# Linear attention and GLU layers on one core: attention read out token by token, key normalization and LayerNorm apply on GpSimd, GLU weights kept, next keys and values emitted between GLU slabs

## The chip, the core and the metric

The kernel runs on one core of one Trainium2 chip. The metric is the device time of one execution in microseconds (us), as a median of several runs. The profile adds the span of one execution, which is some 2 us shorter than the time. Its engines are PE (TensorE products; PEld is its weight load), DVE (VectorE), ACT (ScalarE), POOL (GpSimd) and SP (which issues most DMA transfers).

## The reference

Four layers on 2048 tokens of 512 columns: attention, GLU, attention, GLU, each with a LayerNorm in front and a residual sum behind. Cut to what matters:

```python
# A: 32 heads of 16 columns, linear attention with a softmax feature map
pq, pk = q @ w_phi, k @ w_phi                       # per head, 16x16
phi_q = concat(softmax(pq), softmax(-pq))           # 32 features a head
phi_k = concat(softmax(pk), softmax(-pk))
kv, z = phi_k.T @ v, phi_k.sum(tokens)              # over all tokens
out = (phi_q @ kv) / (phi_q @ z + 1e-6)  ...  @ wo
# B: GLU, F = 1376
h = relu(x @ W_gate) * (x @ W_up);  out = h @ W_down
# layers: x = x + A(ln(x)); x = x + B(ln(x)); twice
```

The sum over all tokens in `kv` is the barrier in an attention layer: no token can be read out before the last key is in.

## The kernel before

The program lists operations with what they read and write and an assumed length. A list scheduler in the file fixes each engine's order from these lengths, before the kernel is built; on the chip every engine then runs its list strictly in order. Tokens come in 16 tiles of 128, or 4 slabs of 512. The parts that matter here (shortened, lambdas unwrapped):

```python
# LayerNorm of a tile: statistics, 1/sqrt by a Newton step, apply: all on DVE; then a DMA transpose
op("dve", tensor_scalar(ytile, x_sb[t], mv[t,0:1], rstd[t], op0=subtract, op1=mult), dur=340)    # L577
dma("sp", dma_start_transpose(yT[:, :, tile], ytile))
...
# keys: exp on ACT, group sums on DVE; VALUES are multiplied by 1/sum, mostly on GpSimd
op("pool", tensor_tensor(vhat[t,s], vsb, rZk[...].to_broadcast([P, 32, 16]), mult), dur=1250)    # L622
...
# query sums, feature-major: 32-column products, reciprocals, transposes, and a 512-column
# product that spreads each head's factor over its 16 rows; the same again for the denominator
op("pe", matmul(pb, EC[c], RT_sb[slab]), dur=216)                                                # L681
op("pe", matmul(pb, kvbd[0,c], expq[st,c,0]), ...); op("pe", matmul(pb, kvbd[1,c], expqm[st,c])) # L727, L729
op("pe", matmul(pb, EC[c], rdenT_sb[slab]), dur=216)                                             # L731
...
# GLU: weights share memory with the attention's buffers and are loaded for each GLU layer
dma("sp", dma_start(Wg, B_W_gate)) ...
# ---- cut: setup, scheduler, semaphores
```

The softmax here doesn't subtract the row's maximum and nothing guards it: scores larger than these inputs give would overflow.

Of the kernel before, what the change touches and what calls it, by code (L numbers as in the profile page):

```python
# [269 lines left out]


class KB:

    def __init__(self, nc, A_x, A_wqkv, A_w_phi, A_wo, B_W_gate, B_W_up, B_W_down, out,
                 nlayers=4, debug_outs=None, dve_vhat_tiles=(2, 5, 7, 10, 13, 15), resid_on_pool=False, ot_mode="half", expqm_mode="half", nr_iters=1, ln_pre_emit=False, rstd_mode="dve", yt_copy_act="half", wcopy_act=True,
                 window=(("sp", 64), ("act", 96), ("pe", 300), ("dve", 24), ("pool", 32)), sched_params=(("SYNC_LAT", 500.0), ("SAME_LAT", 600.0))):
        self.dve_vhat_tiles = tuple(dve_vhat_tiles)
        self.resid_on_pool = resid_on_pool
        self.ot_mode = ot_mode
        self.expqm_mode = expqm_mode  # L280
        self.nr_iters = nr_iters
        self.ln_pre_emit = ln_pre_emit
        self.rstd_mode = rstd_mode
        self.yt_copy_act = yt_copy_act
        self.wcopy_act = wcopy_act
        self.nc = nc
        self.prog = Program(nc, window=dict(window))
        sp = dict(sched_params) if sched_params else {}
        if "SYNC_LAT" in sp:
            self.prog.SYNC_LAT = sp["SYNC_LAT"]  # L290
        if "SAME_LAT" in sp:
            self.prog.SAME_LAT = sp["SAME_LAT"]
        if "DMA_BW" in sp:
            self.prog.DMA_BW = sp["DMA_BW"]
        if "DMA_FIXED" in sp:
            self.prog.DMA_FIXED = sp["DMA_FIXED"]
        if "DMA_GLOBAL_Q" in sp:
            self.prog.DMA_GLOBAL_Q = sp["DMA_GLOBAL_Q"]
        self.A_x, self.A_wqkv, self.A_w_phi, self.A_wo = A_x, A_wqkv, A_w_phi, A_wo
        self.B_W_gate, self.B_W_up, self.B_W_down, self.out = B_W_gate, B_W_up, B_W_down, out  # L300
        self.debug_outs = debug_outs or {}
        self.nlayers = nlayers
        B, S, D = A_x.shape
        assert B == 1 and D == 512 and S % 512 == 0
        self.S = S
        self.NT = S // 128
        self.NSLAB = S // 512
        self.D = 512
        self.NC = 4
        self.H = 32  # L310
        self.DH = 16
        self.HF = 512
        self.F = B_W_gate.shape[1]
        assert self.F == 1376
        self.NFC = 11
        self.FLAST = self.F - 10 * 128
        self.eps_ln = 1e-5
        self.eps_den = 1e-6

    def op(self, eng, fn, reads=(), writes=(), dur=100.0, name=""):  # L320
        return self.prog.op(eng, fn, reads, writes, dur, name)

    def dma(self, eng, fn, reads=(), writes=(), nbytes=0, name=""):
        return self.prog.dma(eng, fn, reads, writes, nbytes, name)

    def build(self):
        nc = self.nc
        S, NT, NSLAB, NC, NFC = self.S, self.NT, self.NSLAB, self.NC, self.NFC
        with ExitStack() as ctx:
            E = ctx.enter_context  # L330
            self.sems = {e: E(nc.semaphore(f"sem_{e}")) for e in ENG_NAMES}
            self.dsems = [E(nc.semaphore(f"dsem{i}")) for i in range(self.prog.n_dma_sems)]

            x_sb = E(nc.sbuf_tensor("x_sb", [P, NT, 512], BF16))
            yT = E(nc.sbuf_tensor("yT", [P, NC, S], BF16))
            wv = E(nc.sbuf_tensor("wv", [P, NC, 512], BF16))
            Wqp = E(nc.sbuf_tensor("Wqp", [P, NC, 512], BF16))
            Wkp = E(nc.sbuf_tensor("Wkp", [P, NC, 512], BF16))
            wo_sb = E(nc.sbuf_tensor("wo_sb", [P, NC, 512], BF16))
            BD = E(nc.sbuf_tensor("BD", [P, NC, 128], BF16))  # L340
            ones_c = E(nc.sbuf_tensor("ones_c", [P, 4, 32], BF16))
            ident = E(nc.sbuf_tensor("ident", [P, 128], BF16))
            ident32 = E(nc.sbuf_tensor("ident32", [P, 128], FP32))
            EC2 = E(nc.sbuf_tensor("EC2", [P, 4, 32], BF16))
            EC2t = E(nc.sbuf_tensor("EC2t", [P, 4, 32], BF16))
            ones32 = E(nc.sbuf_tensor("ones32", [P, 4, 128], BF16))
            EC = E(nc.sbuf_tensor("EC", [P, 4, 128], BF16))
            eps_c = E(nc.sbuf_tensor("eps_c", [P, 1], FP32))
            stats6 = E(nc.sbuf_tensor("stats6", [P, NT, 6], FP32))
            mv = E(nc.sbuf_tensor("mv", [P, NT, 2], FP32))  # L350
            rstd = E(nc.sbuf_tensor("rstd", [P, NT, 1], FP32))
            rs_v1 = E(nc.sbuf_tensor("rs_v1", [P, NT, 1], FP32))
            rs_hx = E(nc.sbuf_tensor("rs_hx", [P, NT, 1], FP32))
            rs_t1 = E(nc.sbuf_tensor("rs_t1", [P, NT, 1], FP32))
            NYB = 6
            ytile = E(nc.sbuf_tensor("ytile", [P, NYB, 512], BF16))
            nA = max(NT * 2 * 512, 2 * NFC * 512, 6144)
            nB = max(NT * 2 * 544, 8 * 1376 + NFC * 512)
            nA = (nA + 511) // 512 * 512
            nB = (nB + 543) // 544 * 544  # L360
            regA = E(nc.sbuf_tensor("regA", [P, nA], BF16))
            regB = E(nc.sbuf_tensor("regB", [P, nB], BF16))
            vsb = E(nc.sbuf_tensor("vsb", [P, 2, 512], BF16))
            Zk = E(nc.sbuf_tensor("Zk", [P, 2, 64], FP32))
            NRZ = 4
            rZk = E(nc.sbuf_tensor("rZk", [P, NRZ, 64], FP32))
            kvbd = E(nc.sbuf_tensor("kvbd", [P, 2, NC, 128], BF16))
            kvden = E(nc.sbuf_tensor("kvden", [P, 2, NC, 32], BF16))
            expq = E(nc.sbuf_tensor("expq", [P, NSLAB, NC, 2, 512], BF16))
            expqm = E(nc.sbuf_tensor("expqm", [P, NSLAB, NC, 512], BF16))  # L370
            rz2tmp = E(nc.sbuf_tensor("rz2tmp", [P, 2, 4, 32], FP32))
            Rtok = E(nc.sbuf_tensor("Rtok", [P, 2, 4, 32], BF16))
            RT_sb = E(nc.sbuf_tensor("RT_sb", [P, S], BF16))
            rden_tmp = E(nc.sbuf_tensor("rden_tmp", [P, 2, 4, 32], FP32))
            rden_tok = E(nc.sbuf_tensor("rden_tok", [P, 2, 4, 32], BF16))
            rdenT_sb = E(nc.sbuf_tensor("rdenT_sb", [P, S], BF16))
            rdenb_sb = E(nc.sbuf_tensor("rdenb_sb", [P, 2, 512], BF16))
            oT = E(nc.sbuf_tensor("oT", [P, 2, NC, 512], BF16))
            numT_sb = E(nc.sbuf_tensor("numT_sb", [P, 2, 512], BF16))
            rbt_sb = E(nc.sbuf_tensor("rbt_sb", [P, 2, 512], BF16))  # L380

            gate_sb = E(nc.sbuf_tensor("gate_sb", [P, 3, 512], BF16))
            pb = [E(nc.psum_tensor(f"pb{i}", [P, 512], FP32)) for i in range(8)]
            pb16 = [pb[i][:].bitcast(BF16) for i in range(8)]
            R_pb = [Res(f"pb{i}", pe_ordered=True) for i in range(8)]

            expk = regA[:, 0:NT * 2 * 512].rearrange("p (t s n) -> p t s n", t=NT, s=2)
            hT = regA[:, 0:2 * NFC * 512].rearrange("p (b f n) -> p b f n", b=2, f=NFC)
            Wqnat = regA[:, 0:2048].rearrange("p (c n) -> p c n", c=4)
            Wknat = regA[:, 2048:4096].rearrange("p (c n) -> p c n", c=4)  # L390
            WT = regA[:, 4096:6144].rearrange("p (c n) -> p c n", c=4)
            vhat = regB[:, 0:NT * 2 * 544].rearrange("p (t s n) -> p t s n", t=NT, s=2)
            Wg = regB[:, 0:4 * 1376].rearrange("p (c n) -> p c n", c=4)
            Wu = regB[:, 4 * 1376:8 * 1376].rearrange("p (c n) -> p c n", c=4)
            Wd = regB[:, 8 * 1376:8 * 1376 + NFC * 512].rearrange("p (c n) -> p c n", c=NFC)

            R = {}

            def RR(key):
                r = R.get(key)  # L400
                if r is None:
                    r = R[key] = Res(str(key))
                return r
            nuA = nA // 512
            nuB = nB // 544
            RA = [Res(f"regA{u}") for u in range(nuA)]
            RB = [Res(f"regB{u}") for u in range(nuB)]

            def uA(e0, e1):
                return [RA[u] for u in range(e0 // 512, (e1 + 511) // 512)]  # L410

# [107 lines left out]
            def R_xall():  # L519
                return [R_x[t] for t in range(NT)]  # L520
# [387 lines left out]
```

## Time and profile before

| | before |
|---|---|
| time, median | 456.97 us (3 runs) |
| span of the profiled run | 453.7 us |
| first GLU product of the two GLU layers | 124.3 and 336.4 us |
| LayerNorm's (LN's) apply: subtract the mean, times 1/root; where and how long | DVE, 0.41 us |

The page first: busy time of each engine, then the busy share in 40 slices of 11.3 us, in tenths (PEclk is the granted TensorE clock), then the engines' shares of the chain that ended last.

```profile
span 453.7 us, 6812 instructions
...
PE 417.4 (92%) x2592; PEld 202.9 (45%) x2592; DVE 298.8 (66%) x696; ACT 174.8 (39%) x317; POOL 92.8 (20%) x128
...
PE   2598989899499999999999999989979999999997
...
DVE  4959984889974333368758999488997333343342
...
POOL 6008660654000000000002666056400000000000
...
PE 72%; DVE 18%; issue 3%; DMA 3%; ACT 2%; POOL 1%; SPq 1%; DVEq 0%; POOLq 0%
```

TensorE is busy for 92% of the span and makes 72% of the chain. GpSimd is idle in both GLU layers (the zeros in its row). The chain in order of time (start, length, engine and line) shows what a GLU layer looks like:

```profile
143.45 0.86 PE pb L779 x4
144.31 0.86 PE pb L782 x4
145.17 9.51 PE pb L794 x44
154.69 0.87 PE pb L779 x4
```

Four 512-column products take 0.86 us and the 44 down products of a slab 9.51, so 216 ns each. A slab takes 28.5 us with no gap, and the four of one layer 114. What can be won lies in the attention layers. The table of stretches (start and end, length, then busy us of PE, PEld, DVE, ACT, POOL with counts, granted clock, DMA) shows the readout of the first attention layer as its second row and a whole GLU layer as its third:

```profile
core 0: us, PE busy (x) PEld busy (x) DVE busy (x) ACT busy (x) POOL busy (x), PEclk, DMA share, GB/s
20.00:76.00 56.00, 52.09 (x385) 28.33 (x385) 44.01 (x98) 40.06 (x77) 24.50 (x40) 1.00 0.19 33
76.00:124.00 48.00, 39.16 (x373) 18.92 (x371) 43.38 (x102) 19.81 (x36) 18.35 (x16) 1.00 0.31 99
124.00:242.00 118.00, 117.67 (x538) 53.76 (x539) 65.18 (x165) 26.49 (x45) 0.00 (x0) 0.99 0.14 27
```

In the readout DVE is busy 43.4 of 48 us and TensorE 39.2. Two groups of instructions matter for later (line, engine, operation, output<-inputs, shapes, count, busy us, mean ns of one, idle time before):

```profile
L577 DVE TENSOR_SCALAR ytile<-x_sb,mv,rstd 128x512 bf16<-128x512 bf16 x64 | 22.7, 406 | 5.6 <-DMA yT<-ytile 5.5
...
L622 POOL TENSOR_TENSOR regB<-vsb,rZk 128x512 bf16<-128x512 bf16 x40 | 41.8, 1058 | 176.8 <-DVE rZk L613 162.5 <-ACT vsb L618 7.9 <-DVE regB L633 2.6
```

### The profile page before, as it was taken

The numbers are of one execution on the slowest core, as the hardware profiler recorded it, in microseconds if no ns is written. First come the engines' busy times: TensorE is split into PE (matmuls) and PEld (weight loads), VectorE is DVE, ScalarE is ACT, GpSimd is POOL, SyncE is SP. The second block draws the span as 40 slices with busy tenths as digits, with TensorE's granted clock in tenths as the row PEclk, the third lists the DMA queues.
The fourth block names the chain that finished last, engine by engine and source line by source line (L and its number), as shares of the span: only waits on it lengthen the run. The fifth ranks groups of instructions, "written<-read, shape, count | busy, mean of one in ns | idle before, by whom it ended". The sixth has DMA issues, their size and how long they took to land.

```text
span 453.7 us, 6812 instructions
## 1 busy us (share of the span) xinstructions
PE 417.4 (92%) x2592; PEld 202.9 (45%) x2592; DVE 298.8 (66%) x696; ACT 174.8 (39%) x317; POOL 92.8 (20%) x128
## 2 busy tenths in 40 slices
PE   2598989899499999999999999989979999999997
PEld 1243458443144444444444345745324444444443
DVE  4959984889974333368758999488997333343342
ACT  3488864445022131231315986435513123131230
POOL 6008660654000000000002666056400000000000
PEclk9999999999989999999999999999999999999999
DMA  8752003610233000002220200370023210100101
GB/s 275 154 94 36 1 1 105 216 58 0 46 72 69 0 2 0 1 0 48 47 46 1 46 1 1 127 237 15 0 56 73 59 48 0 46 1 0 48 1 46
DMA packets 46800, 23.59 MB, mean 52 GB/s; under 512 B 35824, under 2 KB 44720, under 8 KB 46768
## 3 DMA queue, kind: packets, MB, share of 16 engines
q1 hardware_dynamic: 45184, 21.59, 18.6%
q10 hardware_dynamic: 1584, 1.57, 1.0%
q8 instruction: 20, 0.33, 0.3%
q14 instruction: 12, 0.10, 0.1%
HBM read 12.66 MB, written 2.10 MB: 33 GB/s over the span
## 4 chain that ended last, share of the span: by engine, by line
PE 72%; DVE 18%; issue 3%; DMA 3%; ACT 2%; POOL 1%; SPq 1%; DVEq 0%; POOLq 0%
PE pb L779 17%; PE pb L782 17%; PE pb L794 17%; PE pb L604 4%; PE pb L653 4%; PE pb L640 3%; DVE Zk L610 3%; DVE x_sb L757 3%; PE pb L602 2%; DVE regB L630 2%; PE pb L748 2%; DVE stats L530 2%; DMA BD<-in_A_w_phi_dram 2%; DVE expqm L684 1%; PE pb L665 1%
## 5 line engine op out<-in xcount | busy, mean ns | idle before, releaser
L785 ACT ACTIVATE gate_sb<-pb 128x512 bf16<-128x512 f32 (+1 forms) x88 | 52.5, 597 | 176.4 <-PE pb L779 155.8
L787 DVE TENSOR_TENSOR regA<-gate_sb,pb 128x512 bf16<-128x512 bf16 (+1 forms) x88 | 60.3, 686 | 71.4 <-PE pb L782 68.9
L779 PE MATMUL pb<-yT,regB 128*128 128x512 bf16 (+1 forms) x352 | 90.9, 382 | 5.8 <-DMA yT<-ytile 5.8
L782 PE MATMUL pb<-yT,regB 128*128 128x512 bf16 (+1 forms) x352 | 90.9, 382 | 0.0
L622 POOL TENSOR_TENSOR regB<-vsb,rZk 128x512 bf16<-128x512 bf16 x40 | 41.8, 1058 | 176.8 <-DVE rZk L613 162.5
L794 PE MATMUL pb<-regB,regA 128*128 128x512 bf16 (+1 forms) x352 | 77.4, 379 | 0.0
L779 PEld LDWEIGHTS pb<-yT,regB 128*128 128x128 bf16 (+1 forms) x352 | 35.3, 101 | 47.8 <-issue 7.8
L782 PEld LDWEIGHTS pb<-yT,regB 128*128 128x128 bf16 (+1 forms) x352 | 35.5, 101 | 41.3 <-issue 1.1
L794 PEld LDWEIGHTS pb<-regB,regA 128*128 128x128 bf16 (+1 forms) x352 | 34.3, 98 | 41.5
L796 DVE TENSOR_TENSOR x_sb<-x_sb,pb 128x512 bf16<-128x512 bf16 x32 | 22.0, 687 | 46.6 <-PE pb L794 46.6
L530 DVE BATCH_NORM_STATS2 stats<-x_sb 128x6 f32<-128x512 bf16 x64 | 42.5, 671 | 6.3 <-DMA x_sb<-in_A_x_dram 6.3
L656 ACT ACTIVATE expq<-pb 128x512 bf16<-128x512 f32 x64 | 35.7, 613 | 19.9 <-PE pb L653 17.9
L607 ACT ACTIVATE regA<-pb 128x512 bf16<-128x512 f32 x64 | 35.0, 612 | 17.5 <-PE pb L602 17.5
L604 PE MATMUL pb<-wv,yT 128*128 128x512 bf16 x128 | 35.5, 395 | 3.4 <-DVE regB L630 3.3
L610 DVE TENSOR_REDUCE Zk<-regA 128x64 f32<-128x1024 bf16 x32 | 37.8, 1188 | 1.1 <-ACT regA L607 1.1
L748 PE MATMUL pb<-wo_sb,oT 128*128 128x512 bf16 x128 | 32.8, 380 | 5.3 <-DVE x_sb L757 5.3
L602 PE MATMUL pb<-Wkp,yT 128*128 128x512 bf16 x128 | 34.0, 379 | 0.4 <-ACT Wqp L513 0.2
L653 PE MATMUL pb<-yT,Wqp 128*128 128x512 bf16 x128 | 33.5, 379 | 0.0
L577 DVE TENSOR_SCALAR ytile<-x_sb,mv,rstd 128x512 bf16<-128x512 bf16 x64 | 22.7, 406 | 5.6 <-DMA yT<-ytile 5.5
L690 POOL TENSOR_TENSOR expqm<-expq,rbt_sb 128x512 bf16<-128x512 bf16 x16 | 18.5, 1155 | 35.9 <-ACT rbt_sb L688 35.9
L733 ACT ACTIVATE rdenb_sb<-pb 128x512 bf16<-128x512 f32 x32 | 18.4, 597 | 13.8 <-PE pb L731 7.1
L739 POOL TENSOR_TENSOR oT<-rdenb_sb,numT_sb 128x512 bf16<-128x512 bf16 x16 | 18.5, 1155 | 21.9 <-ACT numT_sb L737 15.0
(75 smaller groups left out, 427.2 us busy)
## 6 DMA issues: line engine op xcount, KB each, us to landing
regB<-in_B_W_gate_dram SPq DMA_DIRECT2D x2, 1376.0 KB, 6.0
regB<-in_B_W_up_dram SPq DMA_DIRECT2D x2, 1376.0 KB, 6.0
regB<-in_B_W_down_dram SPq DMA_DIRECT2D x2, 1280.0 KB, 7.0
x_sb<-in_A_x_dram SPq DMA_DIRECT2D x4, 512.0 KB, 9.0
out_dram<-x_sb SPq DMA_DIRECT2D x3, 512.0 KB, 2.9
regA<-in_A_wqkv_dram ACTq DMA_DIRECT2D x2, 512.0 KB, 7.1
yT<-ytile SPq DMA_TRANSPOSE x64, 2.5
wv<-in_A_wqkv_dram ACTq DMA_DIRECT2D x1, 512.0 KB, 11.1
```

The source lines that it names most:

```text
L530: op("dve", (lambda t: (lambda e: e.bn_stats(stats6[:, t, :], x_sb[:, t, :])))(t), reads=[R_x[t]], writes=[R_stats[t]], dur=620, name=f"{t ...
L602: op("pe", (lambda t, ic, bk_k: (lambda e: e.matmul(pb[bk_k][:], yT[:, ic, t * 128:(t + 1) * 128], Wkp[:, ic, :], start=(ic == 0), stop=(i ...
L604: op("pe", (lambda t, ic, bk_v: (lambda e: e.matmul(pb[bk_v][:], yT[:, ic, t * 128:(t + 1) * 128], wv[:, ic, :], start=(ic == 0), stop=(ic ...
L610: op("dve", (lambda t, zb: (lambda e: e.tensor_reduce(Zk[:, zb, :], expk[:, t, :, :].rearrange("p s (h f) -> p (s h) f", f=16), AX.X, ALU. ...
L622: op("pool", (lambda vh, vb, rb, s: (lambda e: e.tensor_tensor(vh[:, :, 0:16], vsb[:, vb, :].rearrange("p (h d) -> p h d", d=16), rZk[:, r ...
L653: op("pe", (lambda st, c, ic, bk: (lambda e: e.matmul(pb[bk][:], Wqp[:, ic, c * 128:(c + 1) * 128], yT[:, ic, st * 512:(st + 1) * 512], st ...
L748: op("pe", (lambda tt, c, bk, ob: (lambda e: e.matmul(pb[bk][:], oT[:, ob, c, tt * 128:(tt + 1) * 128], wo_sb[:, c, :], start=(c == 0), st ...
L779: op("pe", (lambda st, fc, Mf, ic, gb: (lambda e: e.matmul(pb[gb][0:Mf, :], Wg[:, ic, fc * 128:fc * 128 + Mf], yT[:, ic, st * 512:(st + 1) ...
L782: op("pe", (lambda st, fc, Mf, ic, ub: (lambda e: e.matmul(pb[ub][0:Mf, :], Wu[:, ic, fc * 128:fc * 128 + Mf], yT[:, ic, st * 512:(st + 1) ...
L785: op("act", (lambda Mf, gb, gsb: (lambda e: e.activation(gate_sb[0:Mf, gsb, :], pb[gb][0:Mf, :], ACT.Relu)))(Mf, gb, gsb), reads=[R_pb[gb] ...
L787: op("dve", (lambda Mf, ub, gsb, hb, fc: (lambda e: e.tensor_tensor(hT[0:Mf, hb, fc, :], gate_sb[0:Mf, gsb, :], pb[ub][0:Mf, :], ALU.mult) ...
L794: op("pe", (lambda hb, fc, Kf, tt, bk: (lambda e: e.matmul(pb[bk][:], hT[0:Kf, hb, fc, tt * 128:(tt + 1) * 128], Wd[0:Kf, fc, :], start=(f ...
```

## The change

The intent was to take products and DVE work out of the attention readout, and to hide the rest under the GLU, whose products leave the other engines free.

- The readout is token-major: for 128 tokens one product of 144 columns per group gives numerators, denominators and the query sums together. Six small DVE operations, one 1024-element product and a sum of two halves on GpSimd follow; then a DMA transpose in front of the output projection.
- Keys are divided by their sums in place of values, on GpSimd, 1024 elements a tile.
- LayerNorm's reciprocal root and its apply move from DVE to GpSimd.
- The GLU weights have memory of their own and are loaded once.
- The readouts of slabs 1 to 3 and the keys and values of the next attention layer are emitted between GLU slabs.
- The lengths that the scheduler assumes are new as well.

The diff, cut to its core:

```diff
-    op("dve", tensor_scalar(ytile, x_sb[t], mv[t,0:1], rstd[t], op0=subtract, op1=mult), dur=340)
+    op("pool", tensor_scalar(rv1[t], mv[t,1:2], EPS_LN, None, op0=add), 250)                 # L429
+    op("pool", tensor_tensor(rstd[t], rv1[t], mhalf, pow), 300)                              # L430
+    op("pool", tensor_scalar(ytile, x_sb[t], mv[t,0:1], rstd[t], op0=subtract, op1=mult), 600) # L432
 ...
-    op("pool", tensor_tensor(vhat[t,s], vsb, rZk.to_broadcast(...), mult))
+    op("pool", tensor_tensor(expk[t], expk[t], rZk.to_broadcast([P, 64, 16]), mult), 2100)   # L454
 ...
+  def num(t):
+    for g in 8 groups: op("pe", matmul(pb[144 columns], expq[...], kvbd[g]), 66)             # L507
+    op("act", copy to numbf) x3
+    op("dve", zm = tensor_tensor(numbf, numbf, mult), 100) x2                                # L517
+    op("dve", zd = tensor_tensor(zm, zm, add), 100);  op("dve", zr = reciprocal(zd), 330)    # L520, L521
+    op("dve", ab = tensor_tensor(numbf, zr, mult), 100) x2                                   # L523
+    op("dve", tsc = tensor_tensor(numbf, ab.to_broadcast, mult), 620)                        # L527
+    op("pool", osb = tensor_tensor(tsc[0:512], tsc[512:1024], add), 1100)                    # L532
+    dma_start_transpose(oT, osb);  4 x matmul(pb, oT, wo_p);  x_sb += pb                     # L538
 ...
+    N(0); q_proj(1..3); N(1); Bf(0); N(2); Bf(1); N(3); K(0); Bf(2); K(1); Bf(3); K(2) ...
 ---- cut: setup, weight loads, the end
```

## The prediction

> **What bounds it now.** TensorE, in two GLU layers that are packed and two attention layers that are not. In the chain of waits a GLU slab ticks without a gap: 22 groups of four 512-column products at 0.86 us, then 44 down products in 9.51 us: 216 ns each, the warm figure of the Trainium skill ("TensorE: Matmul & The Clock Gate", "Back-to-back issue gap"); 28.5 us a slab, 228 us for both layers. That cannot shrink. The other 220 us: attention until the first GLU product at 124.3 us, and again from about 240 to 336. There the stretch table shows DVE busy 43.4 of the 48 us from 76 to 124, TensorE 39.2.
>
> **Removed.** The 512-column broadcasts of sums (64) and numerators (64): 128 x 216 ns = 28 us of TensorE; 512 32-column products, 64 small transposes; ACT copies of broadcasts, 128x128 reciprocals (0.95 us), DVE's rstd chain and LN apply (0.41 us x64). The second GLU weight load is off the path.
>
> **Added.** 256 144-column products replace the numerators: about 62 ns each, estimated from 59 ns for 136 columns (96 in 5.69 us). Estimated TensorE floor: 1568 x 0.216 + 256 x 0.057 + 16 + 2 = 371 us. On DVE per tile six small ops of 0.15-0.35 us and one 1024-element product, about 0.65 us by "VectorE: DVE Perf Modes", "Rules for kernel authors" (2x on tensor_tensor, bf16 in SBUF); no run yet shows it. GpSimd gets LN's rstd and apply (estimate 1.2 us a tile, from its 0.52 us 128x512 memset and 0.3 us small ops) and the key product, 2 x 1.06 = 2.1 us a tile, from the 128x512 product with a broadcast operand. 32 more DMA transposes (1.27 us issue, 2.5 us to landing) lie between numerator and output projection.
>
> **Moved.** Later readouts go between GLU slabs, three quarters of layer 3's keys and values into and behind slabs 2 and 3. Only the first slab's readout stays exposed.
>
> **The sum (estimates).**
> - Start: weight transposes hold the DMA issuer; first projection about 20 us, before 18.6: no gain.
> - First keys/values: GpSimd bound, 16 x 3.3 us; the issuer is full too. Readout factors ready at about 72; before, the last key product ran at 75.
> - First readout: product, copy, DVE, GpSimd, transpose, projection, LN, transpose, four tiles: 23 us. GLU starts at 95 (before 124).
> - GLU with interleaved work: 114 + 3.5 + 5.5 + 5.5 + 14 = 142, stalls 3: 240. Layer 3 starts when it did, with half its keys done.
> - Eight GpSimd key products in series (17 us) plus latency: factors at 265; readout 21: GLU at 286 (before 336).
> - GLU 128, stalls 3, store 4: span 421; the time is 2 us above the span.
>
> **Predicted: 423 us, 80% range 406 to 440.** Faster by over 2% 0.93, within 2% 0.05, slower 0.02.
>
> **Right if:** GLU's first product comes at 90-100 us and again at 278-295; GpSimd busy rises from 93 to 170-200 us, over 85% between 25 and 70 us and after 243; the key product takes 2.0-2.2 us; the chain of waits goes through GpSimd in those two stretches; a GLU slab with a readout in it takes 33-36 us.
>
> **Wrong if:** GpSimd's one-column power or apply is far over 0.3 and 0.6 us, or the key product slows against DVE; small dependent DVE ops cost over 0.3 us each and stretch the readout; with four banks for gate and up and in-order engines, TensorE stands behind output projections whose inputs are late, losing several us in each of six mixed slabs (towards 440); or start-up is quicker than I think (towards 406).

## The result, and the profile after

The changed kernel gives the right result and takes 487.47 us (485.96 to 487.80, 4 runs), against 456.62 for the kernel before. The ratio is 1.067, 95% interval 1.064 to 1.070: slower by 6.7%, where faster by 7% was predicted. Ratios here are the mean time of one kernel's runs over that of the other's of the same rounds, so not quite the ratio of the medians that are quoted. Executions over 1.5% slower than the fastest of the same kernel are left out of the means. The lines that answer to those of before:

```profile
span 485.6 us, 5893 instructions
...
PE 403.8 (83%) x2112; PEld 192.9 (40%) x2112; DVE 271.2 (56%) x580; ACT 182.1 (38%) x353; POOL 288.2 (59%) x271
...
PE   1626986874999979996689999895699998998997
...
DVE  2731634586742953895366464587563783593342
...
POOL 5999998359560282589999188529490164156000
PEclk9975988996799999999799999997699998999999
...
PE 48%; POOL 32%; DVE 8%; DMA 6%; issue 4%; ACT 3%; ACTq 0%; POOLq 0%
```

TensorE is less busy and DVE too, as intended. GpSimd rose from 92.8 to 288.2 us, far over the predicted 170 to 200, and holds 32% of the chain, where it had 1%. Its row shows nines from the second slice to the sixth, 12 to 73 us. The stretches:

```profile
core 0: us, PE busy (x) PEld busy (x) DVE busy (x) ACT busy (x) POOL busy (x), PEclk, DMA share, GB/s
22.00:84.00 62.00, 41.29 (x226) 20.28 (x225) 24.97 (x33) 26.59 (x51) 60.69 (x51) 0.81 0.39 103
84.00:121.00 37.00, 25.25 (x163) 12.38 (x161) 25.84 (x71) 23.76 (x51) 22.78 (x20) 0.89 0.14 29
121.00:156.00 35.00, 34.81 (x153) 15.65 (x154) 18.02 (x34) 6.97 (x12) 13.73 (x14) 0.92 0.15 31
194.00:240.00 46.00, 36.63 (x179) 16.51 (x177) 29.86 (x75) 16.25 (x32) 37.63 (x38) 0.93 0.19 38
```

From 22 to 84 us GpSimd is busy for 60.7 of 62 us and no other engine is busy for more than 41.3. TensorE idles there, and its granted clock drops to a mean of 0.81. The Trainium skill ("TensorE: Matmul & The Clock Gate", "Part 1: The HAM clock gate") says that the array's clock is cut to half after it stood idle and is restored after some us of work; the trace agrees. The same view in finer stretches, where the first GLU begins:

```profile
117.00:121.00 4.00, 0.00 (x0) 0.00 (x0) 2.15 (x5) 0.56 (x2) 3.79 (x3) 0.50 0.18 37
...
124.00:127.00 3.00, 3.00 (x10) 1.11 (x9) 2.00 (x6) 0.00 (x0) 1.15 (x1) 0.59 0.22 44
127.00:130.00 3.00, 3.00 (x16) 1.35 (x15) 2.65 (x7) 0.60 (x1) 0.63 (x2) 1.00 0.22 44
```

After an idle stretch the clock stands at 0.50, and some 5 us into steady work it is back at 1.00. So the low clock follows from the waiting, and lengthens the first products after it.

The groups of GpSimd, and the one DVE operation that stands out:

```profile
L432 POOL TENSOR_SCALAR ytile<-x_sb,mv,rstd 128x512 bf16<-128x512 bf16 x64 | 133.7, 2092 | 4.5 <-POOL rstd L430 1.6
...
L454 POOL TENSOR_TENSOR expk<-expk,rZk 128x1024 bf16<-128x1024 bf16 x32 | 61.1, 1926 | 7.9 <-DVE rZk L453 7.9
...
L430 POOL TENSOR_TENSOR rstd<-rv,mhalf 128x1 f32<-128x1 f32 x64 | 36.4, 573 | 3.8
...
L520 DVE TENSOR_TENSOR zd<-zm 128x32 f32<-128x32 f32 x32 | 13.3, 415 | 0.6
```

The LN apply takes 2.09 us a tile. I priced it at 0.6 us, and so did the scheduler. It alone is 133.7 us of GpSimd. The chain of waits just before the first GLU product reads:

```profile
110.04 2.09 POOL ytile L432
...
112.41 0.58 POOL rstd L430
...
113.08 2.14 POOL ytile L432
...
115.51 0.58 POOL rstd L430
...
116.18 2.39 POOL ytile L432
...
118.59 2.46 DMA yT<-ytile
```

One apply follows the other every 3.1 us, and only then come the transpose (2.46 us) and the GLU.

### The profile page after: what moved, and what is told of

It is laid out like the page before. It is cut to its first block, busy times and chain, and to the rows that moved or that the text cites. A ratio compares the mean times of both kernels' runs of the same rounds, so it can differ in the third digit from the quotient of the medians.

```text
span 485.6 us, 5893 instructions
## 1 busy us (share of the span) xinstructions
PE 403.8 (83%) x2112; PEld 192.9 (40%) x2112; DVE 271.2 (56%) x580; ACT 182.1 (38%) x353; POOL 288.2 (59%) x271
## 4 chain that ended last, share of the span: by engine, by line
PE 48%; POOL 32%; DVE 8%; DMA 6%; issue 4%; ACT 3%; ACTq 0%; POOLq 0%
PE pb L554 23%; POOL ytile L432 17%; PE pb L568 13%; POOL expk L454 5%; PE pb L443 5%; POOL rstd L430 5%; PE pb L538 3%; DMA oT<-osb 3%; POOL osb L532 2%; POOL rv L429 2%; PE pb L491 2%; DMA yT<-ytile 2%; DVE zd L520 1%; ACT expq L494 1%; DMA hT<-in_A_wqkv_dram 1%
## 5 line engine op out<-in xcount | busy, mean ns | idle before, releaser
L432 POOL TENSOR_SCALAR ytile<-x_sb,mv,rstd 128x512 bf16<-128x512 bf16 x64 | 133.7, 2092 | 4.5 <-POOL rstd L430 1.6
L554 PE MATMUL pb<-yT,Wg 128*128 128x512 bf16 (+1 forms) x352 | 97.0, 389 | 9.4 <-DMA yT<-ytile 9.4
L554 PE MATMUL pb<-yT,Wu 128*128 128x512 bf16 (+1 forms) x352 | 97.0, 388 | 0.1
L532 POOL TENSOR_TENSOR osb<-tsc 128x512 bf16<-128x512 bf16 x32 | 36.8, 1154 | 87.2 <-DVE tsc L527 78.2
L558 DVE TENSOR_TENSOR hT<-gate_sb,pb 128x512 bf16<-128x512 bf16 (+1 forms) x88 | 60.0, 681 | 45.0 <-PE pb L554 43.5
L568 PE MATMUL pb<-Wd,hT 128*128 128x512 bf16 (+1 forms) x352 | 78.4, 381 | 0.0
L451 DVE TENSOR_REDUCE Zk<-expk 128x64 f32<-128x1024 bf16 x32 | 39.0, 1219 | 61.9 <-ACT expk L446 61.7
L511 ACT ACTIVATE numbf<-pb 128x432 bf16<-128x432 f32 (+1 forms) x96 | 43.9, 493 | 65.3 <-PE pb L507 59.0
L454 POOL TENSOR_TENSOR expk<-expk,rZk 128x1024 bf16<-128x1024 bf16 x32 | 61.1, 1926 | 7.9 <-DVE rZk L453 7.9
L430 POOL TENSOR_TENSOR rstd<-rv,mhalf 128x1 f32<-128x1 f32 x64 | 36.4, 573 | 3.8
```

The costliest lines, as they stand in the source:

```text
L430: op("pool", lambda e: e.tensor_tensor(k.rstd[:, t, :], k.rv1[:, t, :], k.mhalf[:], ALU.pow), [r("rv1", t), r("mhalf")], [r("rstd", t)], 3 ...
L432: op("pool", lambda e: e.tensor_scalar(k.ytile[:, yb, :], k.x_sb[:, t, :], k.mv[:, t, 0:1], k.rstd[:, t, :], op0=ALU.subtract, op1=ALU.mul ...
L454: op("pool", lambda e: e.tensor_tensor(k.expk[:, t, :, :].rearrange("p s (h f) -> p (s h) f", f=16), k.expk[:, t, :, :].rearrange("p s (h ...
L511: op("act", (lambda g0, n, bank: lambda e: e.activation(k.numbf[:, b, g0:g0 + n, :], k.pb[bank][:, 0:n * GW].rearrange("p (g m) -> p g m", ...
L532: op("pool", lambda e: e.tensor_tensor(k.osb[:, b, :], k.tsc[:, b, 0:512], k.tsc[:, b, 512:1024], ALU.add), [r("tsc", b)], [r("osb", b)], ...
L554: op("pe", (lambda bank, W, ic, fc, Mf: lambda e: e.matmul(k.pb[bank][0:Mf, :], W[:, ic, fc * 128:fc * 128 + Mf], k.yT[:, ic, st * 512:(st ...
```

## The experiments

"Last key product" means below the last product of keys and values on TensorE (L465; before: L640), the barrier of an attention layer. "GpSimd's key product" is the division of the keys by their sums on L454.

The theories: (1) the apply is slow on GpSimd by itself, and GpSimd is the limit in the exposed stretches. (2) The order is wrong: it was fixed for an apply of 0.6 us, and engines stand behind instructions that it thought ready. (3) The apply is slow because DVE works in the same memory. (4) The new readout chain is what costs, whatever the apply does. Unless another base is named, the edits are to the changed kernel.

### One part undone: the apply on DVE (e1_apply_dve)

```diff
-        op("pool", tensor_scalar(ytile, x_sb, mv, rstd, subtract, mult), 600)
+        op("dve",  tensor_scalar(ytile, x_sb, mv, rstd, subtract, mult), 410)
```

> The change with one part undone: the LN apply runs on DVE again (0.41 us there before the change, 2.09 us on GpSimd after it). Theory 1, the apply's length on GpSimd is what turned the gain into a loss: GpSimd busy falls by about 134 us (288 to 150-160), the first GLU product comes at 95-108 us instead of 122, and again at 285-310 instead of 345; time 425-440 us, faster than the kernel before. Theory 4, the stretched readout (small dependent DVE operations, one more transpose per tile) is what costs: the stretch from the last key product to the first GLU product stays over 35 us and the time stays over 465 us.

Measured: 443.77 us (443.56 to 444.62), ratio 0.973 (0.970 to 0.976): faster than before. GpSimd is busy 156.4 us and the first GLU product comes at 99 us, as theory 1 had it, but the time is above the 425 to 440 us that it expected. The last key product came 20 us earlier, and the readout was only 2.4 us shorter. Theory 4 fails as the main cause, but part of the prediction's gap is left. This order was made anew, so the run doesn't yet separate theories 1 and 2.

The apply on DVE had a surprise: its median is 0.41 us, but the longest took 2.12. Two rows of DVE and one of GpSimd, in order of time (start, length, engine, line):

```profile
199.37 2.12 DVE L432 TENSOR_SCALAR ytile<-x_sb,mv,rstd 128x512 bf16<-128x512 bf16 x1
201.41 1.21 DVE L451 TENSOR_REDUCE Zk<-expk 128x64 f32<-128x1024 bf16 x1
...
199.42 1.93 POOL L454 TENSOR_TENSOR expk<-expk,rZk 128x1024 bf16<-128x1024 bf16 x1
```

The DVE apply ended with GpSimd's key product, within 0.15 us. The Trainium skill ("GPSIMD Engine Reference", "8. Key points") says that GpSimd shares its memory interfaces with VectorE, with contention for some DVE instructions: those in a two-port mode or with two inputs in SBUF. The trace agrees, and shows the size of it: the apply waited until GpSimd's instruction was over. (The records of successive DVE instructions overlap by 0.08 us here, 201.41 against 201.49, so the 0.05 us between the two starts doesn't say which was first.) It goes the other way too. In the changed kernel GpSimd's one-column addition takes 0.22 us as a rule, but from 104.62 us it took 0.63 and ended 0.09 us after a 1024-element product of DVE that had started before it (104.47 to 105.16).

### The right lengths told (e2_true_times)

```diff
-  rstd on GpSimd, 300     apply on GpSimd, 600
+  rstd on GpSimd, 570     apply on GpSimd, 2090
```

> The change as it is, apply and power still on GpSimd, but the scheduler that fixes each engine's order is told their measured lengths (2.09 and 0.57 us instead of 0.6 and 0.3). Theory 2, the loss comes from a wrong order (engines stand behind instructions that the order thought ready): time falls to 445-460 us. Theory 1, the loss is GpSimd's own work in stretches where it is the limit: 475-490 us, GpSimd busy still about 288 us.

Measured: 462.39 us (459.32 to 462.71), ratio 1.012 (1.007 to 1.016), GpSimd busy 288.4 us as in the change. It lies between what the two theories expected. Telling the scheduler the truth won 25 us of the lost time without moving any work to another engine, so theory 2 holds for that part. The gain lies between the first GLU product and the next last key product (192.4 us before, 170.6 now) and after the second one (141.2 and 129.8). TensorE's waits for GpSimd's key product fell from 18.7 to 9.9 us in total; the rest of the gain isn't broken down. The first GLU product still came at 124 us. Moving the apply off GpSimd (the run above) wins another 19 us.

### The disputed cost by itself (e4_probe)

Nine instructions were added to GpSimd's list and one to DVE's, each writing to a dead buffer; the scheduler put them among the last readouts.

```diff
+        op("pool", tensor_scalar(sc, x0, mv, rstd, subtract, mult))   # the apply again
+        op("pool", tensor_scalar(sc, x0, 0.5, 2.0, subtract, mult))   # immediates
+        op("pool", tensor_scalar(sc, x0, rstd, None, mult))           # one operation
+        op("pool", tensor_copy(sc, x0));  tensor_tensor with a broadcast column; of two tiles; ...
```

> The change with some instructions added at its very end that write to dead buffers, each measured alone on GpSimd over 128x512 bf16: the same apply, with immediates for the pointers, with one operation in place of two, a copy, a product with a broadcast column, a product of two tiles, and the apply over 256 columns; and the apply on DVE. Theory 3, the apply is slow because DVE works on the same memory at the time: at the end, where DVE is nearly idle, it takes 0.6-1.2 us. Theory 1, it is slow by itself: 2.05-2.1 us there too; then the variants say whether pointers or the second operation cost (each would halve it), and 256 columns should take about 1.1 us.

Groups of GpSimd (the last one over 256 columns, all others over 512):

```profile
L583 POOL TENSOR_SCALAR tsc<-x_sb,mv,rstd 128x512 bf16<-128x512 bf16 x1 | 2.1, 2075 | 0.1
L584 POOL TENSOR_SCALAR tsc<-x_sb 128x512 bf16<-128x512 bf16 x1 | 1.9, 1938 | 0.1
L585 POOL TENSOR_SCALAR tsc<-x_sb,rstd 128x512 bf16<-128x512 bf16 x1 | 1.6, 1573 | 0.0
L586 POOL TENSOR_SCALAR tsc<-x_sb 128x512 bf16<-128x512 bf16 x1 | 1.5, 1497 | 0.0
...
L589 POOL TENSOR_TENSOR tsc<-x_sb,ytile 128x512 bf16<-128x512 bf16 x1 | 1.2, 1154 | 0.0
...
L587 POOL COPY tsc<-x_sb 128x512 bf16<-128x512 bf16 x1 | 0.6, 611 | 0.0
...
L590 POOL TENSOR_SCALAR tsc<-x_sb,mv,rstd 128x256 bf16<-128x256 bf16 x1 | 1.2, 1222 | 0.0
```

The kernel's time is hardly changed (487.91 us, a single run of unknown state). The apply takes 2.08 us. Pointers cost little: immediates save 0.14 us. Dropping the second operation saves 0.50, not half. Even a multiplication by one immediate takes 1.50 us, more than the product of two tiles (1.15) or of a tile and a broadcast column (1.04). Only the copy takes 0.61 us: the figure that I and the scheduler had used for the apply. From 256 to 512 columns the apply gains 0.85 us, so 3.3 ns an element and some 0.37 us fixed. Theory 3 falls as the main cause: the shortest of the 64 applies in the changed kernel took 2.065 us and the median 2.085, and an effect of DVE would scatter. Only the longest shows something of the kind, with 2.39. (The added instructions ran at 423 to 437 us, before the very end, so the run by itself is not the quiet measurement that the expectation describes; the narrow spread is what decides.) The same apply on DVE took 0.396 us.

### Only this part of the change, on the kernel before (e6_before_apply_pool)

```diff
-                        op("dve", tensor_scalar(ytile, ...), dur=340)
+                        op("pool", tensor_scalar(ytile, ...), dur=2090)
```

> The kernel before with only this part of the change: its LN apply moved to GpSimd, with 2.09 us told to the scheduler. Theory 1: GpSimd busy rises from 93 to about 227 us, and since GpSimd is free in both GLU layers but not in the key/value stretch (2.3 us a tile plus 2.1), the time rises by 8-30 us, to 465-487 us. If the apply's engine hardly matters: within 2% of before.

Measured: 473.57 us (472.08 to 474.90), ratio 1.037 (1.033 to 1.041), GpSimd busy 223.4 us. The apply takes 2.07 us here as well (2.067 to 2.092 for all 64), and alone costs 17 us in a kernel with none of the other changes, in an order made anew. Four applies in a row (8.25 us) stand in the chain ahead of either GLU layer.

### The kernel that the prediction had priced (e7_copy_same_order)

```diff
-        op("pool", tensor_scalar(ytile, x_sb, mv, rstd, subtract, mult), 600)
+        op("pool", tensor_copy(ytile, x_sb), 600)       # wrong result on purpose: 0.61 us
```

The assumed length is the same, so the scheduler makes the same order on every engine. Only the measured length of this instruction differs.

> Wrong result on purpose. The change with each LN apply on GpSimd replaced by a plain copy of the tile there (0.61 us measured, where the apply takes 2.08); the order of all engines stays as it was, made for an apply of 0.6 us. This is the kernel that the prediction priced. If the apply is the only term that failed: GpSimd busy falls by about 95 us to 193, time 420-430 us. If the readout and the start are mis-sized too (as the run with the apply on DVE hints: 29 us from last key product to first GLU product, where 23 and 21 were priced): 435-450 us.

Measured: 435.20 us (432.91 to 436.20), ratio 0.955 (0.951 to 0.958), GpSimd busy 194.3 us, first GLU products at 98 and 299 us (the second outside the predicted 278 to 295). So the 1.48 us that this instruction takes over the 0.6 priced cost 52 us of time (487.5 less 435.2), out of the 64 between predicted and measured. It is the cleanest run here: in the two traces the order of instructions agrees on every engine. The result lies at the edge of its second band, 435 to 450, so a smaller part was mis-sized as well. Its page, and the rows of the two stretches in which the prediction had GpSimd as the limit:

```profile
PE 393.5 (91%) x2112; PEld 189.9 (44%) x2112; DVE 271.7 (63%) x580; ACT 181.6 (42%) x353; POOL 194.3 (45%) x271
...
PE 73%; DMA 9%; DVE 7%; POOL 6%; ACT 3%; issue 1%; ACTq 0%; DVEq 0%; POOLq 0%
...
22.00:70.00 48.00, 41.65 (x264) 21.66 (x262) 27.82 (x36) 30.47 (x58) 40.32 (x38) 0.93 0.54 128
245.00:275.00 30.00, 28.30 (x228) 16.54 (x226) 17.33 (x25) 19.49 (x38) 17.48 (x13) 1.00 0.06 12
```

GpSimd holds 6% of the chain, where it had 32%. In the first stretch TensorE and GpSimd are about equally busy (41.7 and 40.3 of 48 us), and the chain there runs mostly through TensorE and the transposes. In the second TensorE is busy for 28.3 of 30 us and GpSimd for 17.5.

### The interleaving undone (e5_grouped)

On the kernel with the apply on DVE, all readouts were put ahead of the GLU slabs and the next keys behind them.

```diff
-            N(1); Bf(0); N(2); Bf(1); N(3); K(0); Bf(2); K(1); Bf(3); K(2)
+            N(1); N(2); N(3); Bf(0); Bf(1); Bf(2); Bf(3); K(0); K(1); K(2)
```

> The kernel with the apply on DVE (443.8 us), but with the readouts of all four slabs emitted ahead of the GLU slabs and the next keys and values behind them, so the interleaving alone is undone. If the interleaving hides attention work under the GLU: 455-480 us. If it only moves the same waits about: within 2% of 443.8.

Measured: 469.81 us (468.96 to 471.14), ratio to before 1.032 (1.030 to 1.034). Against 443.8 the interleaving is worth 26 us. This part of the change did what it was made for.

### Right lengths and later weights (e9_true_all, e10_late_weights)

Both start from the kernel with the apply on DVE.

```diff
 e9:  -  zm 100, zd 100, ab 100, tsc 620, wv perm 700, issue of a transpose 100
      +  zm 250, zd 415, ab 200, tsc 770, wv perm 1100, issue of a transpose 1270 ...
 e10: -  for _ in range(2 if t >= 2 else 0): emit a weight load
      +  for _ in range(3 if t >= 8 else 0): emit a weight load
```

> The kernel with the apply on DVE, and the scheduler told the measured lengths of everything (small readout operations 0.2-0.42 in place of 0.1 us, issue of a transpose 1.27 in place of 0.1 us). Theory 2 (wrong order) holds for the rest of the gap to the predicted 423: 430-438 us. If the rest is the length of the dependent readout chain: 440-446 us, the stretch from last key product to first GLU product still 27-31 us.

Measured: 443.07 us (441.34 to 444.05), ratio 0.972 (0.969 to 0.975): nothing won. With the apply's length already right, truer lengths for the rest didn't pay here. The readout stretches were 31.4 and 30.1 us.

> The kernel with the apply on DVE, and the GLU and output weights loaded only from the ninth tile on, so that the first transposes don't lie behind them (one pair waited 11.8 us in the chain). If these loads hold up the first stretch: last key product 4-9 us earlier than 70.7 and time 435-440 us. If GpSimd or DVE limits that stretch anyway: within 2 us of 443.8.

Measured: 446.12 us (443.90 to 448.15), ratio 0.979 (0.975 to 0.983): a miss. The last key product came at 73.4 us in place of 70.5, and the first GLU product at 103.5 in place of 98.8.

### The apply on ACT, and weights from ACT's queue (e12_apply_act, e13_act_wq, e14_dve_wq)

```diff
 e12: +  op("pool", -mean*rstd);  op("act", activation(ytile, x_sb, Identity, bias=-mean*rstd, scale=rstd), 600)
 e13, e14: -  dma("sp", weight piece)      +  dma("act", weight piece)
```

All three have the lengths of e9_true_all.

> The LN apply on ACT (a function with scale and bias per row, about 0.6 us; two more one-column products on GpSimd, 0.2 us each), the scheduler told measured lengths. In the run with the apply on DVE the apply took up to 2.1 us where a key product ran on GpSimd (mean 0.65 us against 0.41 before the change). If that waiting costs: 430-437 us and the apply stays at 0.6 us at most. If not: within 3 us of 443.

Measured: 440.35 us (438.64 to 442.66), ratio 0.967 (0.963 to 0.971): 2.7 us better than e9_true_all, just inside the band that says the DVE apply's waiting matters little. The apply takes 0.81 us on ACT, not the 0.6 of the expectation, so this isn't a clean test of that waiting.

> As the run with the apply on ACT, and the GLU and output weights issued from ACT's queue so that transposes don't stand behind them in one queue. If queueing behind the weights holds the first stretch: another 4-9 us off. If not: within 2 us of it.

> The apply on DVE with measured lengths told (443.1 us), weights issued from ACT's queue. If queueing behind the weights holds the first stretch: 434-439 us; if not, within 2 us of 443.

Measured: 447.69 us for e13_act_wq (444.14 to 449.75; ratio 0.982, 0.976 to 0.987), slower than e12_apply_act: its last key product came at 77.5 us, 10.5 later, against the expectation. And 435.02 us for e14_dve_wq (433.43 to 435.22; ratio 0.954, 0.950 to 0.957), the fastest kernel with a right result. The time is as expected, the reason is not: the last key product of the first stretch came at 66.8 us, as in e9_true_all (67.0). The gain of 8 us lies between 99 and 272 us, where e9_true_all's TensorE stood 7.1 us behind output projections that waited for their transposes. In the new order that wait is gone. I take such differences of 5 to 10 us between kernels whose order is made anew for accidents of order; no run shows that, since each changed something else too. Of the runs on the changed kernel, only e7_copy_same_order is free of the doubt.

### The small readout operations taken out (e15_short_readout)

```diff
 on e7_copy_same_order, wrong result on purpose:
-        zm (x2), zd, zr, ab (x2)
+        ab (x2) copied from numbf
```

> Wrong result on purpose. The copy kernel (435.2 us: the apply's cost taken out) with the four small dependent DVE steps of each tile's readout (two products, sum, reciprocal) taken out; two small copies and the 1024-element product stay. In the copy kernel the chain of waits shows 2.7 us of DVE per tile there, and the two stretches from last key product to first GLU product last 29 and 28 us where the prediction had 23 and 21. If these small operations are the other mis-sized term: 2.7 falls to about 1.3 us a tile, the stretches to 22-25 us, time 421-428 us. If the stretch is set by GpSimd, transposes or ACT: 432-436 us.

Measured: 429.50 us (428.32 to 429.62), ratio 0.941 (0.938 to 0.944). The time fell by 5.7 us, less than the 7 to 14 that were expected. The two readout stretches fell from 27.3 and 27.1 us to 23.7 and 24.1, where the prediction had 23 and 21 (counted from a point 1.7 us later, see the sum below). (This order is made anew, so the total is less sure than the stretches.)

### The readout's last sum moved to DVE (e16_sum_dve, e17_act_sum_dve)

What makes these operations long? In the copy kernel's readout, in order of time on DVE, then on GpSimd:

```profile
75.06 0.19 DVE L520 TENSOR_TENSOR zd<-zm 128x32 f32<-128x32 f32 x1
...
76.93 1.04 DVE L520 TENSOR_TENSOR zd<-zm 128x32 f32<-128x32 f32 x1
...
76.77 1.15 POOL L532 TENSOR_TENSOR osb<-tsc 128x512 bf16<-128x512 bf16 x1 [6.74 <-DVE tsc L527]
```

The 32-column sum takes 0.19 us with GpSimd idle. Beside GpSimd's sum of the tile before it takes 1.04 us and ends with it, at 77.9.

```diff
-        op("pool", osb = tensor_tensor(tsc[0:512], tsc[512:1024], add))
+        op("dve",  osb = tensor_tensor(tsc[0:512], tsc[512:1024], add))
```

> The fastest correct kernel so far (apply on DVE, measured lengths told, weights issued from ACT's queue: 435.0 us) with the readout's sum of two halves moved from GpSimd (1.15 us) to DVE. In the copy kernel the 32-column sum of the readout took 1.04-1.10 us where the GpSimd sum of the tile before ran, 0.19 us where GpSimd was idle. If DVE's waiting for GpSimd stretches the readout: the 32-column sum falls to 0.2 us everywhere in the readout, the second stretch from last key product to first GLU product falls by 3-6 us, time 426-432 us. If the chain of small operations is long by itself: within 2 us of 435, as DVE gains the sum's 0.4 us and loses nothing.

> The same on the kernel with the apply on ACT (440.4 us). If DVE's waiting for GpSimd stretches the readout: 431-437 us; if not, 438-442 us.

In e16_sum_dve the same sum, over all 32 tiles (minimum, median and maximum in ns):

```profile
L520 DVE TENSOR_TENSOR zd<-zm x32: 173/185/207, 71.3 to 391.8; 128x32 f32<-128x32 f32 x32
```

It never waits now; in e14_dve_wq its longest took 1.146 us. The waiting is shown. The time went the other way, though: 447.00 us (444.03 to 449.25), ratio 0.978 (0.974 to 0.983). The readout stretches fell only from 32.2 and 30.0 us to 29.3 and 29.4. Between them the new order again let TensorE stand 5.7 us behind output projections, which is part of the loss; the rest isn't explained. e17_act_sum_dve took 437.27 us (436.07 to 438.36), ratio 0.957 (0.955 to 0.960), 3.1 us better than e12_apply_act and a little short of the expected 431 to 437, with the stretches down from 32.1 and 29.9 to 29.8 and 27.1. So without DVE's waiting for GpSimd the exposed readouts of the two runs were 0.6 to 2.9 us shorter, in orders made anew; a gain in time isn't shown.

## Why the prediction was wrong

The step that failed is this one: "GpSimd gets LN's rstd and apply (estimate 1.2 us a tile, from its 0.52 us 128x512 memset and 0.3 us small ops)". Measured were 0.26 for the addition, 0.57 for the power and 2.09 for the apply: 2.9 us a tile. The apply was mis-sized by a factor of 3.5. The prediction named GpSimd as the limit of the first keys and of the stretch after the GLU. In the changed kernel it is the limit of the first (GpSimd busy 60.7 of 62 us), but because of the apply's real length. With the apply near the priced length (e7_copy_same_order) TensorE is as busy there and holds most of the chain, so it is partly luck that the first term came out within 1 us. After the GLU the copy kernel's limit is TensorE (28.3 of 30 us), not GpSimd; in the changed kernel GpSimd was busy for 26.7 of the 36 us from 278 to 314, below the 85% that was forecast, and TensorE for 33.8. The mistake in the failed step was to price an arithmetic operation by a memset, which reads nothing and computes nothing. The prediction listed "GpSimd's one-column power or apply is far over 0.3 and 0.6 us" among what would make it wrong, and gave a slower result 0.02 all the same.

The sum, term by term. As in the prediction, the bounds are the readout factors and the first GLU product (us). The factors are ready 1.7 us after the last key product, so the readouts are by that much shorter here than the stretches quoted above.

| term | predicted | changed kernel | with the copy |
|---|---|---|---|
| start to readout factors | 72 | 92.2 | 72.8 |
| first readout | 23 | 29.0 | 25.6 |
| GLU with readouts and next keys, to the factors | 170 | 194.1 | 175.7 |
| second readout | 21 | 29.1 | 25.4 |
| GLU to the end | 135 | 141.2 | 135.0 |
| span | 421 | 485.6 | 434.5 |

With the copy in the apply's place three of five terms are within 3 us. So:

- Right: start-up wins nothing (first projection at 18.5 us, predicted 20). The GLU slabs keep their 28.5 us (the last one reads 19.00 plus 9.53 us in the chain), and with a readout in them take 34 to 35 us in the copy kernel, as predicted. GpSimd's key product takes 1.93 us, just under the 2.0 to 2.2 priced. The 1024-element product on DVE mostly takes 0.69 us, near the 0.65 that the prediction estimated from the Trainium skill ("VectorE: DVE Perf Modes", "Rules for kernel authors").
- Wrong, and the cause: the apply, 52 of 64 us (shown by e7_copy_same_order against the changed kernel, same order). Of this loss 25 us come back if the scheduler knows the length (e2_true_times), and 19 more if the apply leaves GpSimd (e1_apply_dve). It acts in all five terms: it is GpSimd's own limit ahead of the barrier, four applies in series in each readout, and TensorE standing behind late output projections (15.0 us in all, 6.8 with the copy).
- Wrong, and smaller: the readouts, 25.6 and 25.4 us in place of 23 and 21. In the chain of the copy kernel's readouts the 32-column sum of the second to fourth tile takes 1.03 to 1.10 us beside GpSimd's sum of the tile before, against 0.19 in the first tile: 2.6 us too many in each readout, as much as the whole excess of the first and over half of the second. The two runs without this wait (e16_sum_dve, e17_act_sum_dve) were 0.6 to 2.9 us a readout shorter. Taking out four of the small operations brings the readouts to 22.0 and 22.4, but that removes what had been priced for them too. The prediction feared that the key product would slow against DVE. It didn't (1.92 to 1.99 us in all runs); DVE waits for it, and GpSimd's small operations wait for DVE's long product.
- Wrong, and smaller: the middle term, 175.7 in place of 170. The GLU with its interleaved work takes 146.4 us in the copy kernel, where 145 were predicted. Then come 29.3 us in place of 25. The prediction had eight GpSimd key products in series there; TensorE's own projections and key-value products fill 27.6 of the 29.3 us.
- Open: the other 1.8 us of the second readout, and how the runs with a remade order split into their change and their order. The prediction didn't carry the scatter of remade orders, and no run here repeats one order with only the readout changed.

The idea of the change was sound. The token-major readout, the weights kept and the interleaving, with the apply back on DVE and the weight loads on ACT's queue (e14_dve_wq), run in 435.0 us: 4.6% under before and 10.8% under the change as it was (435.02 over 487.47, medians).

## What to carry to other kernels

Price an instruction on an engine by the same instruction on that engine, or measure it alone before building on it: copy, memset and arithmetic differ more than threefold on GpSimd. Where a static order is made from assumed lengths, one wrong length costs twice, as work and as a bad order for everyone else, so read the real lengths from the first trace and feed them back. When testing a cause in such a kernel, change the instruction's real length and leave its assumed one, and the order stays the same.

## What the Trainium skill lacked or had wrong

- "GPSIMD Engine Reference", "4.1 Engine selection" says that one-input elementwise work on GpSimd is roughly line-rate. That may pass for the copy (0.61 us for 128x512 bf16, a memset 0.52). For arithmetic with a scalar it is wrong: 1.50 us with one operation and an immediate, 1.57 with a pointer, 1.94 with two operations, 2.08 with two pointers, against 0.40 us on DVE and 1.15 us for the product of two tiles on GpSimd itself.
- No page that I found gives the cost of a one-column power on GpSimd: 0.57 us, against 0.20 us for a one-column product.
